# Routed attention and an ELU layer on one core: v asked for ahead of k, k kept in x's columns, weight conversion dealt out by spare time

## The chip, the cores and the metric

The kernel runs on one core of one Trainium2 chip. The metric is the time of one execution in device microseconds (us). Durations and waits below come from one profiled execution.

## The reference, cut to what matters

```python
# q, k, v: (4, 8, 768, 64) float32; centroids: (8, 16, 64) float32
q_assign = argmax(einsum('bhsd,hcd->bhsc', q_n, c_n)); k_assign = argmax(einsum(... k_n, c_n))
scores = where(q_assign == k_assign, q @ k.T / 8, -1e9)        # per batch and head
x = (softmax(scores) @ v)                                       # 4*768 = 3072 tokens x 512
h = x @ w_in                                                    # w_in: (512, 2048)
out = where(h > 0, h, exp(min(h, 0)) - 1) @ w_out               # w_out: (2048, 512)
```

The two weights arrive as float64, so the kernel itself has to turn them into float32.

## The kernel before, in words

**Attention.** The work is cut into 32 *slots*: for each of 4 batches, 2 halves of 384 queries, and 4 pairs of heads (`blocks`, line 153). `slot(n)` (line 555) records one slot on all engines in a fixed order; every engine runs its own instructions in the order recorded. In slot n TensorE does the row sums of slot n-2 (`row_sums`, L500, `d_bank`), the product with v of slot n-1 (`values`, L482, `o_bank`), in some slots the match of the next queries or keys with the centroids (`similar`, L373), and then for six blocks of keys the scores (`plain`, L444) and the cluster mask added to them (`masked`, L457), in a ring of three PSUM tiles. ScalarE takes the exponentials of the six score tiles (L466) into `p_out`, which has one buffer: the first exponential of slot n+1 overwrites what VectorE adds up in `sums_begin` (L469) of slot n. VectorE's queue in a slot holds `sums_end` of slot n-1 (L474, L475), `divide` of slot n-2 (L514, L515), `assign` where clusters are matched (L386 to L399), transposes of the next batch's k and q (L580, L587, L591), then `weigh(n)` (line 595), then `sums_begin` of slot n (L469). GpSimd multiplies x by the reciprocal sums (L518) and makes the query masks (L409).

**Loads.** SyncE's queue issues all loads. In each slot it holds the k loads (`load_k`, 4 transfers for each pair of heads) or the q loads (`load_q`, 16 transfers) of the next batch first, and behind them `load_v(n + 1)` (line 594). v has two buffers, so the v of slot n+1 may be written once `values(n - 1)` has read the buffer. At the start SyncE asks for the centroids, the first q, the first k (8 transfers), v of slot 0, the other half of q, and then four pieces of weights (L300).

**Weight conversion.** The weights are cut into 16 pieces of 1 MB (8 of w_in, then 8 of w_out). A piece is loaded as words into a *place*: `words_w` (to the end), two places in columns of `xT` and one in `spare` (the last three only up to some piece). `begin` is two VectorE instructions (L319, L327) and one for ScalarE behind the slot's exponentials (L329, through `later` and `flush`); `join` is three VectorE instructions (L338, L341, L344). After them the place is free, and `ask` (line 279) records the load of the next piece into it. A table `order` written by hand says which slot has a begin ("b") or a join ("j"). It runs on through four more steps, the four *units* of the first group of the second stage: pieces 13, 14 and 15 are begun and joined there.

**Second stage.** Tokens come in six groups of 512. Each group has four units (`unit`, L666: seven block products with w_in, summed in a way that saves the eighth) and a `second_product` with w_out (L758). Sums of blocks are needed as operands: of x (`x_sums`, L627 to L630, GpSimd), of w_in (`sum_low`, L639, and `w_step`, L646 to L650, GpSimd) and of w_out (`weight_sums`, L814 to L817, VectorE, once, in the first group after its four units). In a unit VectorE adds m5 to a bank (L713), which TensorE's sixth product then adds to, and u3 to another (L723); the rest of a unit's VectorE work (`rest_of`) stands at the start of the next.

## Time and profile before

| | us |
|---|---|
| median of three runs (987.08 to 990.1) | 989.21 |
| the profiled execution, its own time | 989.96 |
| its span | 988.2 |
| TensorE busy in the span | 933.7 |
| VectorE, ScalarE, GpSimd busy | 530.3, 371.1, 279.8 |

The span runs from 0 to 988.2. The slots end near 373.6, the first group of the second stage runs to 496.6, and the other groups take 96.7 each. In a timeline row the first number is the start, the second the duration in us; then come engine, line, operation, tiles, how many instructions the row merges, and in brackets how long the engine had been idle and what ended that. SPq is SyncE's queue, whose rows are the issuing of transfers and not their data. PEclk is the clock that TensorE was granted, in tenths.

### The profile page before, as it was taken

The numbers are of one execution on the slowest core, as the hardware profiler recorded it, in microseconds if no ns is written. First come the engines' busy times: TensorE is split into PE (matmuls) and PEld (weight loads), VectorE is DVE, ScalarE is ACT, GpSimd is POOL, SyncE is SP. The second block draws the span as 40 slices with busy tenths as digits, with TensorE's granted clock in tenths as the row PEclk, the third lists the DMA queues.
The fourth block names the chain that finished last, engine by engine and source line by source line (L and its number), as shares of the span: only waits on it lengthen the run. The fifth ranks groups of instructions, "written<-read, shape, count | busy, mean of one in ns | idle before, by whom it ended". The sixth has DMA issues, their size and how long they took to land.

```text
span 988.2 us, 12274 instructions
## 1 busy us (share of the span) xinstructions
PE 933.7 (94%) x4905; PEld 674.8 (68%) x4907; DVE 530.3 (54%) x638; ACT 371.1 (38%) x619; POOL 279.8 (28%) x251
## 2 busy tenths in 40 slices
PE   6699999999899979877999999999999999999996
PEld 3244444444344437766888888888888888888885
DVE  4768899889788986756134213422441244214321
ACT  3567877577577754320033103300330032003200
POOL 1102020221203174627034504440444043405200
PEclk9899999999999989987999999999999999999999
DMA  6853535434322211110000000000000100010001
GB/s 141 238 139 81 119 69 117 121 73 109 79 76 91 76 59 43 45 41 1 22 22 1 1 21 22 1 1 24 20 1 1 42 1 1 0 43 1 1 1 45
DMA packets 107983, 49.13 MB, mean 50 GB/s; under 512 B 93200, under 2 KB 101392, under 8 KB 107280
## 3 DMA queue, kind: packets, MB, share of 16 engines
q1 hardware_dynamic: 107920, 48.28, 18.5%
q8 instruction: 40, 0.66, 0.3%
q14 instruction: 23, 0.19, 0.1%
HBM read 41.98 MB, written 6.29 MB: 49 GB/s over the span
## 4 chain that ended last, share of the span: by engine, by line
PE 80%; DVE 9%; issue 3%; DMA 3%; SPq 3%; POOL 1%; ACT 1%; DVEq 0%; POOLq 0%
PE bank L758 29%; PE bank L666 21%; PE o_bank L482 10%; PE banks L444 9%; PE o_bank L666 4%; SPq L163 3%; PE banks L457 2%; PE d_bank L666 2%; PE d_bank L500 2%; DMA kq_g<-in_v_dram 2%; DVE sums_w L474 1%; PE d_bank L373 1%; DMA words_w<-in_moe_w_out_dram 1%; DVE sums_w L469 1%; POOL kq_g L677 1%
## 5 line engine op out<-in xcount | busy, mean ns | idle before, releaser
L758 PE MATMUL bank<-w_out,kq_g 128*128 128x256 f32 x768 | 172.0, 384 | 8.4 <-DVE w_out L815 8.4
L758 PEld LDWEIGHTS bank<-w_out,kq_g 128*128 128x128 f32 x768 | 148.0, 193 | 29.2 <-DVE w_out L815 8.5
L466 ACT ACTIVATE p_out<-banks 128x768 f32<-128x768 f32 x192 | 154.6, 812 | 27.8 <-PE banks L457 27.7
L482 PE MATMUL o_bank<-p_out,kq_g 128*64 128x384 f32 x768 | 135.3, 503 | 14.9 <-DMA kq_g<-in_v_dram 14.9
L482 PEld LDWEIGHTS o_bank<-p_out,kq_g 128*64 128x64 f32 x768 | 56.4, 142 | 89.2 <-issue 66.5
L677 POOL TENSOR_SCALAR kq_g<-kq_g 128x512 f32<-128x512 f32 x96 | 63.1, 667 | 170.0 <-ACT kq_g L676 169.8
L680 DVE SCALAR_TENSOR_TENSOR kq_g<-kq_g,bank 128x512 f32<-128x512 f32 x72 | 49.4, 686 | 115.3 <-POOL kq_g L677 115.3
L518 POOL TENSOR_TENSOR xT<-xT,sums_w 128x384 f32<-128x384 f32 x32 | 36.7, 1146 | 228.7 <-DVE sums_w L515 212.6
L666 PE MATMUL bank<-xT,w_in 128*128 128x256 f32 x384 | 90.7, 379 | 0.1
L646 POOL TENSOR_TENSOR spare<-w_in 128x512 f32<-128x512 f32 x24 | 33.5, 1395 | 179.9 <-PE bank L666 177.0
L666 PEld LDWEIGHTS bank<-xT,w_in 128*128 128x128 f32 x384 | 73.0, 190 | 10.1
L666 PE MATMUL bank<-xT,spare 128*128 128x256 f32 x288 | 69.7, 394 | 7.3 <-ACT bank L712 4.0
L469 DVE TENSOR_TENSOR sums_w<-p_out 128x1536 f32<-128x1536 f32 x32 | 57.1, 1786 | 21.0 <-ACT p_out L466 21.0
L666 PE MATMUL bank<-x_sum,w_in 128*128 128x256 f32 x288 | 68.0, 379 | 0.0
L666 PEld LDWEIGHTS bank<-xT,spare 128*128 128x128 f32 x288 | 56.8, 198 | 16.3 <-POOL kq_g L677 8.1
L474 DVE TENSOR_TENSOR sums_w<-sums_w,p_out 128x1536 f32<-128x1536 f32 x32 | 58.3, 1823 | 3.3
L666 PEld LDWEIGHTS bank<-x_sum,w_in 128*128 128x128 f32 x288 | 54.7, 190 | 7.4
L676 ACT ACTIVATE kq_g<-bank 128x512 f32<-128x512 f32 x72 | 42.0, 598 | 38.6 <-PE bank L666 36.9
L705 ACT COPY bank<-bank 128x512 f32<-128x512 f32 x12 | 6.8, 570 | 125.3 <-PE bank L666 125.3
L409 POOL TENSOR_SCALAR kq_g<-w_out,big,minus 128x768 bf16<-128x768 bf16 x16 | 28.6, 1793 | 72.3 <-ACT w_out L402 72.3
L444 PE MATMUL banks<-kq_g 64*128 64x384 f32 x192 | 41.8, 515 | 5.3 <-ACT p_out L466 5.3
L758 PE MATMUL bank<-sums_w,p_out 128*128 128x256 f32 x192 | 42.4, 379 | 0.0
(162 smaller groups left out, 1388.3 us busy)
## 6 DMA issues: line engine op xcount, KB each, us to landing
kq_g<-in_v_dram SPq DMA_DIRECT2D x32, 384.0 KB, 3.4
words_w<-in_moe_w_out_dram SPq DMA_DIRECT2D x6, 1024.0 KB, 5.1
out_dram<-p_out SPq DMA_DIRECT2D x24, 256.0 KB, 2.3
w_out<-in_q_dram SPq DMA_DIRECT2D x112, 48.0 KB, 2.4
w_out<-in_k_dram SPq DMA_DIRECT2D x48, 96.0 KB, 3.2
words_w<-in_moe_w_in_dram SPq DMA_DIRECT2D x3, 1024.0 KB, 5.6
xT<-in_moe_w_in_dram SPq DMA_DIRECT2D x3, 1024.0 KB, 8.5
spare<-in_moe_w_in_dram SPq DMA_DIRECT2D x2, 1024.0 KB, 10.2
```

The costliest lines, as they stand in the source:

```text
L444: nc.tensor.matmul(s[:, e, :HS], lhsT=kT[b % 2][pr][rows, ts(kt, P)], rhs=qT[half][pr][rows], start=True, stop=False,)
L466: nc.scalar.activation(probs[kt], s[:, :, :HS], Act.Exp, scale=SCALE)
L469: nc.vector.tensor_tensor(add_to, probs_all[:, : 4 * HS], probs_all[:, 4 * HS : 8 * HS], op=Alu.add)
L474: nc.vector.tensor_tensor(add_to, add_to, probs_all[:, 8 * HS :], op=Alu.add)
L482: nc.tensor.matmul(o_bank[64 * e : 64 * e + 64, :HS], lhsT=v_raw[n % 2][:, e, kt], rhs=probs[kt][:, e], start=(kt == 0), stop=(kt == NT - 1),)
L518: nc.gpsimd.tensor_tensor(x_of(n), x_of(n), r_of, op=Alu.mult)
L646: nc.gpsimd.tensor_tensor(s2, s1, a11, op=Alu.subtract)
L666: nc.tensor.matmul(bank[:, ts(f, QS)], lhsT=left[:, ch, ts(f, P)], rhs=right[:, ch], start=first and f == 0 and ch == 0, stop=ch == 1, ski ...
L676: nc.scalar.activation(to, bank.rearrange("p (f n) -> p f n", f=2), Act.Exp)
L677: nc.gpsimd.tensor_scalar(to, to, 1.0, 0.0, op0=Alu.min, op1=Alu.max)
L680: nc.vector.scalar_tensor_tensor(to, to, -1.0, bank.rearrange("p (f n) -> p f n", f=2), op0=Alu.add, op1=Alu.max)
L758: nc.tensor.matmul(bank[:, ts(i, QS)], lhsT=left[:, f, ts(i, P)], rhs=right[:, f], start=first and f == 0 and i == 0, stop=f == half - 1, ...
```

## The change

Six things are changed.

1. `load_v(n + 1)` stands ahead of a slot's k and q loads.
2. The first k is asked for by ScalarE: four transfers as its first instructions, four more after its second table load. Its copies out of PSUM are shared by ScalarE and VectorE, the centroids are transposed after q, and the mask columns of the second half of k are copied by ScalarE after the first three exponentials of slot 0.
3. k of batches 0 and 2 is kept in the last 768 columns of `xT` rather than in the first 3072 columns of `w_out`'s tile (`early`). The places for words are now `words_w`, the first 2048 columns of `early` (for pieces 0 to 7) and `spare` (to piece 9); for piece 13 alone there is one more, the last 2048 columns of `early`, from slot 25 on.
4. The table `order` is replaced by a rule: each slot brings an amount of spare time (`ROOM`), unused time is carried on up to 2.5, and begin, join and sum steps are taken in order as long as the credit pays their `COST`. A join is now three steps that may fall into different slots, and the place is given back after the second of them. By this rule all 16 pieces are begun by slot 30 and joined by slot 31 but for the last step of piece 15 (after unit 0).
5. The sums of w_out are four steps of the same list: three after unit 2, one after unit 3. Tiles `words_w` and `sums_w` change roles in them.
6. `sum_low` is gone: after slot 25 GpSimd issues two transfers from `w_in` into `w_in` that add as they write. The first group's x sums and w sums are dealt over slots 27 to 30, where they stood together after slot 30.

The core of the diff:

```diff
-        [early[:, ts(pr, S)] for pr in range(NPR)],
+        [xT[:, pr, N - S :] for pr in range(NPR)],
...
-    first_k = [
-        rows_of(t, k[0, 2 * pr : 2 * pr + 2])
-        for pr, t in enumerate(raw_k + kT[1][2:])
-    ]
+    def load_first_k(pr):
+        first_k[pr] = rows_of(nc.scalar, (raw_k + kT[1][2:])[pr], k[0, 2 * pr : 2 * pr + 2])
+
+    load_first_k(0)
+    load_first_k(1)
     load_v(0)
     load_q(0, 1)
...
     nc.scalar.preload_act_table_set("natural_log_exp_and_others")
+    load_first_k(2)
+    load_first_k(3)
...
-    places += [(xT[:, 2 * n : 2 * n + 2, N - WC :], 6) for n in range(KC // 2)]
-    places += [(spare.rearrange("p a n -> p (a n)")[:, : 2 * WC].unsqueeze(1), into + 4)]
+    places += [(early[:, : 2 * WC].unsqueeze(1), into)]
+    places += [(spare.rearrange("p a n -> p (a n)")[:, : 2 * WC].unsqueeze(1), into + 2)]
...
-        order[n] = ("", "j", "b", "j", "b", "", "j", "b")[n % NB]
...
+        [2.3, 2.6, 3.0, 3.0, 1.4, 1.7, 2.6, 2.6] * (B - 1)
...
+    COST = {"begin": 1.4, "join": 1.25, "sum": 2.2}
...
+        credit = min(credit, 2.5) + ROOM[n]
+        begun = False
+        while steps and credit >= COST[steps[0][0]]:
+            kind, m = steps[0]
+            if kind == "join" and begun or kind == "sum" and n < len(blocks) + 2:
+                return
...
-        nc.scalar.copy(kT[0][pr].rearrange("p (h s) -> p h s", h=2), ps[:, :, :HS])
+        copy = nc.vector.tensor_copy if pr % 2 else nc.scalar.copy
+        copy(kT[0][pr].rearrange("p (h s) -> p h s", h=2), ps[:, :, :HS])
...
-    for other in told:
-        other()
+    told[0]()
     flush()
+    told[1]()
...
+        if n + 1 < len(blocks):
+            load_v(n + 1)
         if at == 0:
             nc.vector.transpose(qT_all[1], raw_q_all)
...
-        if n + 1 < len(blocks):
-            load_v(n + 1)
         weigh(n)
...
-            if k_ == 0:
-                sum_low(u + 1)
             w_step(u + 1, 0)
...
-        if n == last_n - 1:
-            x_sums(0, nc.gpsimd)
-            sum_low(0)
-            for m in range(3):
-                w_step(0, m)
+        if n == 3 * NB + 1:
+            places.append((early[:, 6144:].unsqueeze(1), into + 6))
+            ask()
+            for ch in range(2):
+                nc.gpsimd.dma_start(
+                    w_in[:, ch, DF // 2 :], w_in[:, 2 + ch, DF // 2 :], accum_op=Alu.add
+                )
+        elif last_n - 4 <= n < last_n:
+            x_sum_step(0, n - last_n + 4)
+            if n > last_n - 4:
+                w_step(0, n - last_n + 3)
```

Three places show how the instructions move. The first is SyncE's queue from the first q to slot 1. `in_q`, `in_k`, `in_v` and `in_moe_w_in` are the inputs in memory, `kq_g` holds v's two buffers, and `words_w`, `xT`, `w_out` and `spare` hold places for words. Before:

```order
L189 DMA p_out<-in_q_dram 128x3x64 x8
L189 DMA w_out<-in_k_dram 128x6x64 x4
L189 DMA kq_g<-in_k_dram 128x6x64 x4
L179 DMA kq_g<-in_v_dram 128x2x384
L163 DMA w_out<-in_q_dram 32x12x32 x16
L300 DMA words_w<-in_moe_w_in_dram 128x2048
L300 DMA xT<-in_moe_w_in_dram 128x2x1024 x2
L300 DMA spare<-in_moe_w_in_dram 128x2048
L163 DMA w_out<-in_k_dram 32x24x32 x8
L179 DMA kq_g<-in_v_dram 128x2x384
L163 DMA w_out<-in_q_dram 32x12x32 x16
```

And after, the same stretch of SyncE's queue:

```order
L189 DMA p_out<-in_q_dram 128x3x64 x8
L179 DMA kq_g<-in_v_dram 128x2x384
L163 DMA w_out<-in_q_dram 32x12x32 x16
L303 DMA words_w<-in_moe_w_in_dram 128x2048
L303 DMA w_out<-in_moe_w_in_dram 128x2048
L303 DMA spare<-in_moe_w_in_dram 128x2048
L179 DMA kq_g<-in_v_dram 128x2x384
L163 DMA w_out<-in_k_dram 32x24x32 x8
L179 DMA kq_g<-in_v_dram 128x2x384
L163 DMA w_out<-in_q_dram 32x12x32 x16
```

The first k has left the queue, three pieces of weights are asked for where there were four, and the v of slot 1 stands ahead of the next batch's k.

The second place is VectorE in slot 30, with slot 29's `sums_begin` ahead of it. Before:

```order
L469 TENSOR_TENSOR sums_w<-p_out 128x1536
L474 TENSOR_TENSOR sums_w<-sums_w,p_out 128x1536
L475 TENSOR_TENSOR sums_w<-sums_w 128x768
L514 TENSOR_TENSOR sums_w<-sums_w 128x384
L515 SCALAR_TENSOR_TENSOR sums_w,r_sum<-sums_w 128x384
L338 SCALAR_TENSOR_TENSOR sums_w<-words_w,sums_w 128x1024
L341 SCALAR_TENSOR_TENSOR w_out<-words_w,w_out 128x1024
L344 SCALAR_TENSOR_TENSOR w_out<-w_out,sums_w 128x1024
L319 TENSOR_SCALAR w_out<-words_w 128x1024
L327 TENSOR_SCALAR sums_w<-words_w 128x1024
L469 TENSOR_TENSOR sums_w<-p_out 128x1536
```

And after, where the join is of piece 14 and the begin of piece 15:

```order
L510 TENSOR_TENSOR sums_w<-p_out 128x1536
L515 TENSOR_TENSOR sums_w<-sums_w,p_out 128x1536
L516 TENSOR_TENSOR sums_w<-sums_w 128x768
L555 TENSOR_TENSOR sums_w<-sums_w 128x384
L556 SCALAR_TENSOR_TENSOR sums_w,r_sum<-sums_w 128x384
L342 SCALAR_TENSOR_TENSOR sums_w<-words_w,sums_w 128x1024
L346 SCALAR_TENSOR_TENSOR w_out<-words_w,w_out 128x1024
L352 SCALAR_TENSOR_TENSOR w_out<-w_out,sums_w 128x1024
L322 TENSOR_SCALAR w_out<-words_w 128x1024
L330 TENSOR_SCALAR sums_w<-words_w 128x1024
L510 TENSOR_TENSOR sums_w<-p_out 128x1536
```

The rows are the same: both times a join out of `words_w` is followed at once by a begin out of `words_w`, with the load of the next piece between them.

The third place is VectorE at the border of units 2 and 3 of the first group. Before, with the join of piece 14 and the begin that waits for the words of piece 15:

```order
L713 TENSOR_TENSOR bank_2403<-bank_2403,spare 128x512
L680 SCALAR_TENSOR_TENSOR kq_g<-kq_g,bank_2402 128x2x256
L723 TENSOR_TENSOR bank_2405<-bank_2405,spare 128x512
L338 SCALAR_TENSOR_TENSOR sums_w<-words_w,sums_w 128x1024
L341 SCALAR_TENSOR_TENSOR w_out<-words_w,w_out 128x1024
L344 SCALAR_TENSOR_TENSOR w_out<-w_out,sums_w 128x1024
L319 TENSOR_SCALAR w_out<-words_w 128x1024
L327 TENSOR_SCALAR sums_w<-words_w 128x1024
L680 SCALAR_TENSOR_TENSOR kq_g<-kq_g,bank_2403 128x2x256
```

And after:

```order
L757 TENSOR_TENSOR bank_2423<-bank_2423,spare 128x512
L724 SCALAR_TENSOR_TENSOR kq_g<-kq_g,bank_2422 128x2x256
L765 TENSOR_TENSOR bank_2425<-bank_2425,spare 128x512
L362 TENSOR_TENSOR sums_w<-w_out 128x2048
L364 TENSOR_TENSOR w_out<-w_out 128x8x256
L366 TENSOR_TENSOR sums_w<-w_out,sums_w 128x2048
L724 SCALAR_TENSOR_TENSOR kq_g<-kq_g,bank_2423 128x2x256
```

Join and begin have given way to three sums of w_out, which wait for no load; the four sums that stood after unit 3 are no longer there.

More of the change, by code (lines that the diff above doesn't have):

```diff
@@ L532, in main_path @@
                 nc.vector.tensor_copy(qT[0][pr], ps[:, e, :HS])
-    told = clusters_q(0, 0, d_bank)
-    told()
+    nc.tensor.transpose(o_bank[:, :P], work[:, : 2 * D], ident)
+    nc.vector.tensor_copy(cT, o_bank[:, :P])
+    clusters_q(0, 0, d_bank)()
     flush()
```

121 lines of the change are left out of this document (73 added, 48 removed).

## The prediction

> **What bounds the kernel now.** I read the page's slices first, then the busy time by stage, then who waited for whom, then the timeline of the engine that waits.
>
> ```profile
> PE   6699999999899979877999999999999999999996
> ```
>
> TensorE is busy nearly throughout; the slices that fall short lie in the first 20, that is, before about 494. The busy times of three stretches (TensorE's comes first, VectorE's third; then the granted clock) say how much is there.
>
> ```profile
> 53.20:373.60 320.40, 307.51 (x2018) 141.77 (x2016) 284.07 (x315) 226.17 (x367) 72.00 (x49) 0.98 0.37 93
> 373.60:496.60 123.00, 107.18 (x459) 91.15 (x460) 66.31 (x74) 24.41 (x43) 51.62 (x37) 0.92 0.08 30
> 496.60:593.30 96.70, 96.70 (x449) 85.13 (x449) 30.19 (x39) 19.79 (x35) 31.85 (x32) 1.00 0.03 12
> ```
>
> The second group of the second stage (third row) has no wait at all: 96.70 busy of 96.70, at full clock. The first group does the same products in 123.00, so 26.3 us of it are waits and slow clock. From the second group on nothing can be gained by this change, which leaves that work alone. The rest of the loss lies in the slots, and the waits name it.
>
> ```profile
> PE o_bank L482 <- DMA kq_g<-in_v_dram: 14.9, 4, 7.3
> PE bank L758 <- DVE w_out L815: 8.4, 1, 8.4
> PE banks L444 <- ACT p_out L466: 8.1, 2, 5.3
> PE bank L666 <- POOL kq_g L677: 3.3, 1, 3.3
> ```
>
> So TensorE waits four times for v, twice for exponentials, and in the first group for the sums of w_out and once for GpSimd.
>
> **v ahead of k (a gain).** TensorE's timeline around those four waits, with an undisturbed slot between them:
>
> ```profile
> 46.60 6.65 PE L482 MATMUL o_bank<-p_out,kq_g 128*64 128x384 f32 x24 [7.35 <-DMA kq_g<-in_v_dram]
> 67.94 0.87 PE L500 MATMUL d_bank<-sums_w,ones 128*64 128x384 f32 x4
> 68.64 4.04 PE L482 MATMUL o_bank<-p_out,kq_g 128*64 128x384 f32 x24
> 77.65 0.87 PE L500 MATMUL d_bank<-sums_w,ones 128*64 128x384 f32 x4
> 90.58 4.09 PE L482 MATMUL o_bank<-p_out,kq_g 128*64 128x384 f32 x24 [1.57 <-DMA kq_g<-in_v_dram]
> 174.16 5.79 PE L482 MATMUL o_bank<-p_out,kq_g 128*64 128x384 f32 x24 [2.54 <-DMA kq_g<-in_v_dram]
> 260.40 2.19 PE L482 MATMUL o_bank<-p_out,kq_g 128*64 128x384 f32 x6 [3.50 <-DMA kq_g<-in_v_dram]
> ```
>
> An undisturbed slot lasts 77.65 - 67.94 = 9.71, and its product with v 4.04. After the waits of 7.35 and 2.54 that product takes 6.65 and 5.79, at a slower clock: 2.6 and 1.75 more; after 1.57 it does not (4.09). For the fourth wait, longer than the third, I take the third's 1.75. The four cost 14.9 + 2.6 + 1.75 + 1.75 = 21.0.
>
> Why v is late stands in SyncE's queue:
>
> ```profile
> 27.25 14.82 SPq L163 DMA_DIRECT2D w_out<-in_k_dram  x8
> 42.11 0.65 SPq L179 DMA_DIRECT2D kq_g<-in_v_dram  x1
> 76.18 10.60 SPq L163 DMA_DIRECT2D w_out<-in_q_dram  x16
> 86.88 8.21 SPq L179 DMA_DIRECT2D kq_g<-in_v_dram  x3
> ```
>
> Eight k transfers take 14.82 to be asked for, and v only then, at 42.11; it is wanted near 39 and its product starts at 46.60. Later, v stands behind sixteen q transfers (10.60). With v first, each is asked for some 10 us earlier, and the largest wait was 7.35, so all four go: -21.0. What v is moved past comes later instead: v's request waits until the product of the slot before last has read the buffer, some 5 us into the slot (0.7 + 4.04), and k or q behind it by as much. They are turned two or three slots later, 19 us or more, so this costs nothing; if that cover were gone it would be up to 5 us in a slot.
>
> **Conversion dealt out: the slots.** Pieces 13 to 15 move into the slots. Their prices, from VectorE's timeline:
>
> ```profile
> 97.86 1.18 DVE L338 SCALAR_TENSOR_TENSOR sums_w<-xT,sums_w 128x1024 uint32<-128x1024 uint32 x1
> 101.35 1.75 DVE L469 TENSOR_TENSOR sums_w<-p_out 128x1536 f32<-128x1536 f32 x1
> 107.02 0.58 DVE L386 STREAM_TRANSPOSE w_out<-d_bank 128x384 f32<-128x384 f32 x1
> 109.32 0.65 DVE L319 TENSOR_SCALAR w_in<-xT 128x1024 uint32<-128x1024 uint32 x1
> 110.49 1.75 DVE L469 TENSOR_TENSOR sums_w<-p_out 128x1536 f32<-128x1536 f32 x1
> ```
>
> A join runs from 97.86 to 101.35, 3.49; the fixed sums of a slot from there to 107.02, 5.67; matching clusters to 109.32, 2.30; a begin to 110.49, 1.17. Joins that meet GpSimd's multiplication, which the divide ahead of them sets off, are dearer (the second step 2.02 below, where a third of 3.49 is 1.2), about 4.3. Three more pieces are 3 x 5.5 = 16.5, so VectorE goes from 284.07 to about 300 in a stretch that without v's waits lasts some 309. It fits on the whole, by 8 us, and the rule keeps each slot near its spare 9.71 - 5.67 = 4.0. I put the moved joins at nothing, with the cover of 8 us named; without it see the second rival.
>
> One wait stays. In slot 30 the rows before and after are the same: a join frees `words_w`, the next piece is loaded into it, and the begin stands right behind.
>
> ```profile
> 348.73 1.22 DVE L338 SCALAR_TENSOR_TENSOR sums_w<-words_w,sums_w 128x1024 uint32<-128x1024 uint32 x1
> 349.87 2.02 DVE L341 SCALAR_TENSOR_TENSOR w_out<-words_w,w_out 128x1024 f32<-128x1024 uint32 x1
> 356.94 1.29 DVE L319 TENSOR_SCALAR w_out<-words_w 128x1024 uint32<-128x1024 uint32 x1 [2.84 <-DMA words_w<-in_moe_w_out_dram]
> 359.82 2.85 DVE L469 TENSOR_TENSOR sums_w<-p_out 128x1536 f32<-128x1536 f32 x1
> 359.94 1.15 ACT L329 ACTIVATE sums_w<-sums_w,off 128x1024 uint32<-128x1024 uint32 x1 [8.02 <-DVE sums_w L327]
> 363.63 1.65 PE L444 MATMUL banks<-kq_g 64*128 64x384 f32 x4 [5.28 <-ACT p_out L466]
> ```
>
> The load takes 356.94 - 351.89 = 5.05. Join and begin last 359.82 - 348.73 = 11.1; queued behind them are VectorE's sum and ScalarE's L329 with all its exponentials, and TensorE waits 5.28, then loses about 2.6 to the clock as after the 7.35: 7.9. After the change GpSimd's eight sums no longer fall into the begin (359.82 - 356.94 = 2.88 there, 1.17 alone): 1.7 less. Slots 27 to 29 bring the steps of before in another order (5.5, 4.3 and 1.2 where 4.3, 1.2 and 5.5 stood), which would bring VectorE to slot 30 earlier, and two of GpSimd's sums each, which slow it; I take the two as cancelling. The wait is then 5.28 - 1.7 = 3.6, and its clock loss, between the 1.75 after 2.54 and the 2.6 after 7.35, about 2.2: 5.8, a gain of 2.1 (bounds: all 7.9 gained, or 3 lost).
>
> The Trainium skill ("TensorE: Matmul & The Clock Gate", "Part 1: The HAM clock gate") says that the clock falls to half after an idle window of about 3.4 us. This trace slows after 2.54 already, so a wait between 2.5 and 3.4 would cost 1.75 by the trace and nothing by the page.
>
> **Conversion and sums: the first group (a gain).** Two of the places where the 26.3 us go, and what the sums of w_out cost:
>
> ```profile
> 424.00 0.69 DVE L319 TENSOR_SCALAR w_out<-words_w 128x1024 uint32<-128x1024 uint32 x1 [3.66 <-DMA words_w<-in_moe_w_out_dram]
> 428.07 3.75 PE L666 MATMUL bank<-xT,spare 128*128 128x256 f32 x8 [4.00 <-ACT bank L712]
> 451.88 4.63 PE L758 MATMUL bank<-w_out,kq_g 128*128 128x256 f32 x10 [8.40 <-DVE w_out L815]
> ```
>
> VectorE waits for words at 424.00; behind it stand its additions to the banks, and TensorE waits 4.00 at 428.07 (and 3.3 in the unit before, with GpSimd between). The four sums then hold it for 8.40: 15.7 together. The remaining 10.5 are 107.18 busy against 96.70: slow clock after these waits and 0.9 of row sums. After the change no load and no begin is left here. What stays: the row sums, 0.9, about as much again for the first unit's start (an estimate), and a new, smaller wait, for three sums now stand between L723 of unit 2 and the L713 of unit 3. The same two units of the second group, undisturbed:
>
> ```profile
> 530.11 0.70 DVE L723 TENSOR_TENSOR bank<-bank,spare 128x512 f32<-128x512 f32 x1 [0.38 <-ACT spare L721]
> 538.73 0.70 DVE L713 TENSOR_TENSOR o_bank<-o_bank,spare 128x512 f32<-128x512 f32 x1 [1.61 <-ACT bank L712]
> 541.32 1.89 PE L666 MATMUL o_bank<-xT,spare 128*128 128x256 f32 x8
> ```
>
> VectorE is free at 530.8. A sum of 2048 columns is 1.75 x 2048/1536 = 2.33, three are 7.0, and 1.6 more if two of GpSimd's operations meet them at the 0.8 of above; the rest of the unit behind them is five operations of 0.7, and L713 another 0.7: done at 543.6. TensorE wants it at 541.32: it waits 2.3 (0 to 3.5), and I add half of 1.75 for the clock. The first group lasts 96.7 + 1.8 + 2.3 + 0.9 = 101.7: -21.3 (bounds -18 to -24.5).
>
> **The block added by a transfer.** No row shows such a transfer; the nearest are 1 MB loads. It is issued after slot 25 and first needed by the w sums after slot 28, about 29 us later, on GpSimd, behind which x's multiplications are queued. At nothing it is hidden by those 29 us; GpSimd is rid of four sums of blocks, for which TensorE never waited longer than the 3.3 above.
>
> **First k by ScalarE (a loss).**
>
> ```profile
> 6.44 0.48 ACT L530 COPY x_sum<-banks 128x384 f32<-128x384 f32 x1 [1.68 <-PE banks L526]
> 6.56 2.69 SPq L189 DMA_DIRECT2D w_out<-in_k_dram  x4
> 25.07 4.40 ACT L466 ACTIVATE p_out<-banks 128x768 f32<-128x768 f32 x6
> ```
>
> No row shows ScalarE asking. By SyncE's row four requests take 2.69, and two such groups, 5.4, now stand in ScalarE's queue ahead of its copy of q at 6.44. ScalarE has some of that time free (1.68 just ahead of the copy), so I let the copy move by 2.4 (bounds 0 and 5.4), and all that follows with it. Sharing the k copies, and putting half of the mask copies behind three exponentials, gives most of it back by the first exponential (25.07), but that half, about 1.0, then stands among the six. Net +1.5 (-1.5 if requests cost ScalarE nothing, +3.4 if nothing is given back). SyncE's later loads are asked for that much sooner, which only v needs.
>
> The Trainium skill ("DMA: Bandwidth & Descriptors", "Issuing engines are not separate DMA queues") says that asking from several engines saves only the time to ask. By the page this part could gain no more than that time; the row gives it as 2.69 for four, and it is not saved but moved to ScalarE.
>
> **Sum.** -21.0 - 2.1 - 21.3 + 1.5 = -42.9. The profiled execution took 989.96, its span 988.2 and 1.8 around it; it would come to 947.1. It lies 0.75 above the median, 989.21, and against that I forecast 946.
>
> **Rivals.**
> 1. *The left waits go too* (0.12): slot 30's load lands in time and the sums hide behind the unit. For it: an exponential of the next slot needs VectorE's sum only some 5 us into that slot. Against: the same rows in slot 30. 5.8 + 3.2 less: 937.
> 2. *VectorE becomes the bound of the slots* (0.18): if GpSimd's work meets each step, as it did at 349.87, eight joins of w_in and sixteen begins cost 0.8 more each: 19, of which 8 is covered: 11 more, 957. For it: 300 of 309. Against: the join quoted above cost 3.49.
> 3. *v does not come sooner at the start* (0.10), so the change does less than it says: three pieces of weights are still ahead of the first v. The queue stood 14.82 over eight k requests with four pieces ahead; if the data and not the asking was the limit, and is still, the 10 us of the first wait stay: 956. Against: one piece and all of k have gone from ahead of v.
> 4. *The adding transfer is late* (0.03), slower than before: GpSimd stops at the first w sum, and x's multiplications behind it, ScalarE and TensorE follow within a slot. It decides from 29 + 43 = 72 us after its issue; at 100 us the kernel takes 946 + 71 = 1017. Against: the slowest group of loads of 1 MB lands 10.2 after its issue in the median:
>
> ```profile
> spare<-in_moe_w_in_dram SPq DMA_DIRECT2D x2, 1024.0 KB, 10.2
> ```
>
> The Trainium skill ("SBUF — State Buffer", "SBUF: two separate sides") says that a transfer issued from GpSimd can stand while VectorE holds the port through which GpSimd writes its descriptors. No run here shows one.
>
> **How the numbers follow.** My forecast has 0.57, the rivals 0.12, 0.18, 0.10 and 0.03. The range 936 to 961 holds the first three rivals and the bounds of slot 30, of the start and of the first group, each by itself; outside lie the fourth rival and several bad bounds at once. A difference under 0.3% (3 us) can't be told from none. Faster 0.96, same 0.01, slower 0.03.
>
> **What would show it.** In the new profile: no wait of the product with v, and slots of 9.71 (more where clusters are matched) from slot 1 to 29; one wait of TensorE for an exponential near slot 31, of 2 to 6; a first group of 100 to 104 with a wait in unit 3; the first exponentials at 25 to 27. It is wrong if the slots grow beyond 9.71 with VectorE busy throughout, if v's wait is back in slot 2, or if GpSimd waits for its transfer.

## The result and the profile after

The kernel after takes **956.02 us** (median of 4 runs, 955.51 to 957.19), the kernel before 988.14 in the runs beside it (986.79 to 990.1): a ratio of 0.9675, with a 95% interval of 0.9653 to 0.9697. That is 32 less where the forecast was 43 less. It lies inside the range given, but in the sum behind it one term has the wrong sign and one is far too small, while two hold. The profiled execution took 955.51, of which the span is 953.7.

TensorE's row of the slices is the first thing to set beside the one of before: the short slices of the slots have gone, but for the very first and one 7, from 334 to 358, where slot 30 lies.

```profile
PE   3999999999999979999999999999999999999996
```

The first digit was 6 and is 3, and that is about the start. The loads and waits of five stretches say the rest (TensorE's busy time first, VectorE's third, then the granted clock): the start up to the first product with v, the slots, the last slots, the first group of the second stage, and the second group.

```profile
0.00:35.40 35.40, 18.09 (x97) 10.31 (x97) 16.00 (x41) 10.71 (x17) 2.70 (x9) 1.00 0.96 223
35.40:307.00 271.60, 271.60 (x1830) 126.16 (x1828) 261.26 (x304) 207.08 (x334) 61.53 (x42) 1.00 0.48 117
307.00:361.00 54.00, 45.65 (x288) 20.79 (x284) 50.00 (x42) 30.79 (x53) 23.10 (x12) 0.94 0.21 70
...
361.32:462.10 100.78, 99.08 (x460) 85.63 (x459) 44.41 (x58) 21.64 (x40) 39.28 (x34) 1.00 0.02 6
462.10:558.80 96.70, 96.70 (x449) 85.13 (x449) 30.20 (x39) 19.78 (x35) 31.78 (x32) 1.00 0.03 12
```

From 35.4 to 307 TensorE has no idle time at all and VectorE is busy 261 of 272. In the last slots TensorE lacks 8.35 and some clock; in the first group 1.7.

**The start.** Before, TensorE reached the first product with v at 28.54:

```profile
28.54 4.09 PE L482 MATMUL o_bank<-p_out,kq_g 128*64 128x384 f32 x24
```

ScalarE's queue after, from the first instruction, and that product on TensorE:

```profile
0.76 4.51 ACTq L189 DMA_DIRECT2D w_out<-in_k_dram  x4
...
6.81 1.28 ACT L242 ACT_TABLE_LOAD   x1
10.12 4.12 ACTq L189 DMA_DIRECT2D kq_g<-in_k_dram  x4
14.29 0.48 ACT L571 COPY x_sum<-banks 128x384 f32<-128x384 f32 x1 [6.19 <-DMA w_out<-in_q_dram]
35.41 4.09 PE L523 MATMUL o_bank<-p_out,kq_g 128*64 128x384 f32 x24
```

Four requests take ScalarE 4.51 and 4.12, and between the table load, done at 8.09, and the second four stands a gap of 2.03, for which the rows name no reason. The first copy of q (L571; it was L530) starts at 14.29 instead of 6.44, and the product with v at 35.41: **6.9 later**, where 1.5 was forecast.

**The slots.** Three lines of TensorE's waits after; none of its waits names v any more. (`L485` is the old `L444`, `L507` the exponentials, `L757` the additions to the banks.)

```profile
PE banks L485 <- ACT p_out L507: 8.9, 4, 6.0
PE banks L567 <- ACT x_sum L571: 8.4, 2, 7.8
PE o_bank L710 <- DVE o_bank L757: 1.7, 1, 1.7
```

The first blank matmul behind attention starts at 361.32 instead of 373.63, 12.3 sooner. The slots can be read from the starts of TensorE's row sums, one in each slot. Before, those of slots 27, 30 and 31; after, those of slots 27 to 31:

```profile
321.85 0.87 PE L500 MATMUL d_bank<-sums_w,ones 128*64 128x384 f32 x4
...
350.99 0.87 PE L500 MATMUL d_bank<-sums_w,ones 128*64 128x384 f32 x4
368.73 1.10 PE L500 MATMUL d_bank<-sums_w,ones 128*64 128x384 f32 x4
```

```profile
307.16 0.87 PE L541 MATMUL d_bank<-sums_w,ones 128*64 128x384 f32 x4
318.40 0.87 PE L541 MATMUL d_bank<-sums_w,ones 128*64 128x384 f32 x4
329.48 0.87 PE L541 MATMUL d_bank<-sums_w,ones 128*64 128x384 f32 x4
339.19 0.87 PE L541 MATMUL d_bank<-sums_w,ones 128*64 128x384 f32 x4
356.65 0.87 PE L541 MATMUL d_bank<-sums_w,ones 128*64 128x384 f32 x4
```

From the first product with v to the row sums of slot 27 it is 293.3 before (28.54 to 321.85) and 271.75 after (35.41 to 307.16): **21.6 gained** for v, against 21.0. A slot is 9.71. Before, slot 30 was too long by 8.0 (17.74), and slot 31 took 0.2 more to the blank matmul (4.90, where after has 4.67); after, slots 27, 28 and 30 are too long, by 1.53, 1.37 and 7.75, together 10.65: **2.4 more**, where 2.1 less was forecast. With the 6.9 of the start, 21.6 - 2.4 - 6.9 makes up the 12.3.

VectorE, ScalarE and TensorE around the long slot:

```profile
339.48 1.22 DVE L342 SCALAR_TENSOR_TENSOR sums_w<-words_w,sums_w 128x1024 uint32<-128x1024 uint32 x1
340.62 2.02 DVE L346 SCALAR_TENSOR_TENSOR w_out<-words_w,w_out 128x1024 f32<-128x1024 uint32 x1
342.67 2.18 DVE L352 SCALAR_TENSOR_TENSOR w_out<-w_out,sums_w 128x1024 f32<-128x1024 f32 x1
347.67 0.70 DVE L322 TENSOR_SCALAR w_out<-words_w 128x1024 uint32<-128x1024 uint32 x1 [2.82 <-DMA words_w<-in_moe_w_out_dram]
349.00 1.15 ACT L332 ACTIVATE sums_w<-sums_w,off 128x1024 uint32<-128x1024 uint32 x1 [8.89 <-DVE sums_w L330]
352.54 1.65 PE L485 MATMUL banks<-kq_g 64*128 64x384 f32 x4 [5.99 <-ACT p_out L507]
```

From the join's start to the end of the begin, at 348.9, it is now 9.4 instead of 11.1, as forecast. But the join starts 0.3 behind the slot's row sums (339.19), where before it started 2.3 ahead of them (348.73 and 350.99): VectorE comes to it 2.5 later, not sooner.

**The first group** lasts 100.78 instead of 122.97: **22.2 gained**, against 21.3. VectorE's sums of w_out, the next addition to a bank, and TensorE behind it, in units 2 and 3:

```profile
397.48 2.28 DVE L362 TENSOR_TENSOR sums_w<-w_out 128x2048 f32<-128x2048 f32 x1
399.79 2.58 DVE L364 TENSOR_TENSOR w_out<-w_out 128x2048 f32<-128x2048 f32 x1
402.29 2.69 DVE L366 TENSOR_TENSOR sums_w<-w_out,sums_w 128x2048 f32<-128x2048 f32 x1
409.11 0.69 DVE L757 TENSOR_TENSOR o_bank<-o_bank,spare 128x512 f32<-128x512 f32 x1
409.94 1.97 PE L710 MATMUL o_bank<-xT,spare 128*128 128x256 f32 x8 [1.70 <-DVE o_bank L757]
```

The three sums end at 404.98, 7.5 behind their start, and the one wait that is left is 1.70, in unit 3, where 2.3 was forecast; its clock loss is small (1.97 for a product of 1.89).

The four parts, -21.6, +2.4, -22.2 and +6.9, add up to -34.5, the difference of the two spans (988.2 and 953.7). It is more than the 32 of the medians because the profiled execution of before, 989.96, was one of its longer ones, and that of after its shortest.

### The profile page after: what moved, and what is told of

It is laid out like the page before. It is cut to its first block, busy times and chain, and to the rows that moved or that the text cites. A ratio compares the mean times of both kernels' runs of the same rounds, so it can differ in the third digit from the quotient of the medians.

```text
span 953.7 us, 12273 instructions
## 1 busy us (share of the span) xinstructions
PE 918.4 (96%) x4907; PEld 668.3 (70%) x4907; DVE 523.1 (55%) x640; ACT 369.1 (39%) x617; POOL 274.9 (29%) x249
## 3 DMA queue, kind: packets, MB, share of 16 engines
q1 hardware_dynamic: 101264, 46.71, 18.5%
## 4 chain that ended last, share of the span: by engine, by line
PE 81%; DVE 13%; DMA 2%; ACT 1%; SPq 1%; issue 1%; DVEq 0%; ACTq 0%
PE bank L796 30%; PE bank L710 23%; PE banks L485 8%; PE o_bank L523 8%; PE o_bank L710 4%; DVE sums_w L515 2%; PE banks L498 2%; PE d_bank L710 2%; PE d_bank L541 2%; DVE sums_w L510 2%; DVE sums_w L516 1%; SPq L163 1%; DVE w_out L352 1%; PE d_bank L414 1%; DVE w_out L346 1%
## 5 line engine op out<-in xcount | busy, mean ns | idle before, releaser
L796 PE MATMUL bank<-w_out,kq_g 128*128 128x256 f32 x768 | 169.0, 379 | 0.0
L507 ACT ACTIVATE p_out<-banks 128x768 f32<-128x768 f32 x192 | 153.7, 813 | 27.6 <-PE banks L498 22.5
L796 PEld LDWEIGHTS bank<-w_out,kq_g 128*128 128x128 f32 x768 | 145.8, 190 | 19.8
L523 PE MATMUL o_bank<-p_out,kq_g 128*64 128x384 f32 x768 | 129.3, 486 | 0.0
L710 PE MATMUL bank<-xT,spare 128*128 128x256 f32 x288 | 66.1, 379 | 0.0
L515 DVE TENSOR_TENSOR sums_w<-sums_w,p_out 128x1536 f32<-128x1536 f32 x32 | 61.0, 1907 | 3.7 <-ACT sums_w L551 0.5
L710 PEld LDWEIGHTS bank<-xT,spare 128*128 128x128 f32 x288 | 54.7, 190 | 7.4
L450 POOL TENSOR_SCALAR kq_g<-w_out,big,minus 128x768 bf16<-128x768 bf16 x16 | 35.0, 2193 | 64.6 <-ACT w_out L443 64.6
L485 PE MATMUL banks<-kq_g 64*128 64x384 f32 x192 | 41.3, 510 | 8.3 <-ACT p_out L507 8.3
L796 PE MATMUL bank<-sums_w,kq_g 128*128 128x256 f32 x192 | 42.4, 379 | 0.0
```

Of the source, the lines that this page charges most:

```text
L450: nc.gpsimd.tensor_scalar(q_mask[half][:, :, x], hot_q, big[:, x : x + 1], minus[:, x : x + 1], op0=Alu.mult, op1=Alu.add,)
L485: nc.tensor.matmul(s[:, e, :HS], lhsT=kT[b % 2][pr][rows, ts(kt, P)], rhs=qT[half][pr][rows], start=True, stop=False,)
L507: nc.scalar.activation(probs[kt], s[:, :, :HS], Act.Exp, scale=SCALE)
L515: nc.vector.tensor_tensor(add_to, add_to, probs_all[:, 8 * HS :], op=Alu.add)
L523: nc.tensor.matmul(o_bank[64 * e : 64 * e + 64, :HS], lhsT=v_raw[n % 2][:, e, kt], rhs=probs[kt][:, e], start=(kt == 0), stop=(kt == NT - 1),)
L710: nc.tensor.matmul(bank[:, ts(f, QS)], lhsT=left[:, ch, ts(f, P)], rhs=right[:, ch], start=first and f == 0 and ch == 0, stop=ch == 1, ski ...
```

## The experiments

The kernels ran in five sets, each on one chip with runs of the kernel before in between; these had medians of 986.45 to 989.05, so a difference of 1 to 2 between kernels of two sets tells nothing. The medians, and the ratios to the kernel before in the same set (the sets are parted by the empty rows):

| kernel | median us | ratio (95%) |
|---|---|---|
| the change | 956.02 | 0.9675 (0.9653 to 0.9697) |
| | | |
| first k by SyncE | 953.33 | 0.9669 (0.9639 to 0.9700) |
| second k group behind the copies | 949.81 | 0.9623 (0.9602 to 0.9643) |
| begin not in the slot of its load | 951.11 | 0.9629 (0.9604 to 0.9653) |
| before, with v ahead alone | 968.54 | 0.9803 (0.9770 to 0.9835) |
| | | |
| first k by GpSimd | 953.91 | 0.9658 (0.9636 to 0.9680) |
| k by SyncE, first begin in slot 1 | 946.81 | 0.9581 (0.9560 to 0.9603) |
| sums of w_out at the end | 964.15 | 0.9756 (0.9734 to 0.9778) |
| lower block added by GpSimd | 957.13 | 0.9686 (0.9664 to 0.9708) |
| | | |
| first begin in slot 1 alone | 954.81 | 0.9676 (0.9651 to 0.9701) |
| three edits together | 940.75 | 0.9535 (0.9510 to 0.9560) |
| the three, joins spread | 940.18 | 0.9527 (0.9502 to 0.9552) |
| | | |
| as the last, k by GpSimd | 944.28 | 0.9561 (0.9541 to 0.9581) |

The theory to be tested: the sum fell short by the start (ScalarE's queue) and by the last slots (a begin behind its own load); its rivals are that transfers, whoever asks for them, set the start, and that VectorE as a whole sets the last slots.

### First k by SyncE again

```diff
-    load_first_k(0)
-    load_first_k(1)
+    for pr in range(NPR):
+        load_first_k(pr)
     load_v(0)
...
-        first_k[pr] = rows_of(nc.scalar, (raw_k + kT[1][2:])[pr], k[0, 2 * pr : 2 * pr + 2])
+        first_k[pr] = rows_of(nc.sync, (raw_k + kT[1][2:])[pr], k[0, 2 * pr : 2 * pr + 2])
```

> The changed kernel with one part undone: SyncE asks for all eight transfers of the first k again, behind the first q and ahead of v. Theory A (asking holds ScalarE: its two groups of requests, 4.51 and 4.12 with a gap of 2.03 ahead of the second, stand ahead of its first copy of q, which starts at 14.29 instead of 6.44): the copy is back between 6.4 and 7.5, the first product with v starts at 29 to 30 instead of 35.41, and the kernel takes 950 (949 to 951.5) instead of 956. Theory B (the transfers themselves fill the DMA engines from 4 us on, whoever asks): the first product with v stays near 35, and the kernel takes 955 to 958.

Measured: 953.33, between the two (its runs spread from 951.53 to 956.95). ScalarE's first copy, the first product with v, and what came behind:

```profile
5.56 0.48 ACT L569 COPY x_sum<-banks 128x384 f32<-128x384 f32 x1 [0.86 <-PE banks L565]
29.12 2.16 PE L521 MATMUL o_bank<-p_out,kq_g 128*64 128x384 f32 x12
31.44 1.15 ACT L330 ACTIVATE sums_w<-sums_w,off 128x1024 uint32<-128x1024 uint32 x1 [5.41 <-DVE sums_w L328]
33.34 2.27 PE L521 MATMUL o_bank<-p_out,kq_g 128*64 128x384 f32 x12 [2.06 <-ACT p_out L505]
```

The copy and the product are back where theory A wants them, 6.3 sooner. But SyncE now gets to the words at 24.55 instead of 19.23, the first begin waits for them in slot 0, and its step on ScalarE (L330) stands ahead of exponentials that the product needs: TensorE waits 2.06 in the middle of it. From 25.5 to 29.1 the granted clock was 0.53 as well. So asking from ScalarE did buy something, 5.3 of SyncE's time, which the forecast had put at nothing.

### The second k group behind the copies of q

```diff
     nc.scalar.preload_act_table_set("natural_log_exp_and_others")
-    load_first_k(2)
-    load_first_k(3)
...
+    load_first_k(2)
+    load_first_k(3)
     nc.tensor.transpose(o_bank[:, :P], work[:, : 2 * D], ident)
```

> The changed kernel with ScalarE's second group of four k requests behind its two copies of the first q instead of ahead of them. Theory A: the first copy starts at about 8.2, when the table load ends; the second group is then asked for from about 10.8 to 15 and lands near 19, where its transposes would want it near 17, so the first product with v starts at 31 to 32.5 and the kernel takes 952.5 (951.5 to 954). Theory B (the transfers fill the DMA engines): 955 to 958.

Measured: 949.81, more than theory A hoped for, because the second group landed all but in time (its transposes wait 0.4).

```profile
8.01 0.48 ACT L569 COPY x_sum<-banks 128x384 f32<-128x384 f32 x1
11.61 2.81 ACTq L189 DMA_DIRECT2D kq_g<-in_k_dram  x4
29.80 4.09 PE L521 MATMUL o_bank<-p_out,kq_g 128*64 128x384 f32 x24
```

The copy starts as the table load ends, and the product at 29.80, 5.6 sooner than in the change. The place of four requests ahead of two copies, with the gap ahead of them, thus cost 5.6. Behind the copies the same four requests took 2.81, not 4.12.

### No begin in the slot of its load

```diff
+        first_unasked = asked
+        fresh = range(first_unasked, len(pieces))
         while steps and credit >= COST[steps[0][0]]:
             kind, m = steps[0]
+            if kind == "begin" and m in fresh:
+                return
```

> The changed kernel with one rule more in the dealing out: a block of words isn't begun in the slot in which it was asked for, so that the begin of block 15 moves from slot 30 to slot 31 and its three joins behind the first unit of the first group. Theory A (TensorE's wait of 5.99 in slot 30 is the begin's wait for words, with the exponentials queued behind it): the wait goes, slot 30 lasts 9.7 to 10.5 instead of 17.46, up to 2 comes back in the first group, and the kernel takes 949.5 (948 to 951). Theory B (VectorE is late by the three joins of each of the slots 27, 28 and 30 anyway, and the 2.82 that it waits for words is all there is to gain): 953 (952.5 to 954).

Measured: 951.11, between the two. The wait of 5.99 is gone, and in the same slot this one stands:

```profile
348.54 1.09 PE L489 MATMUL banks<-kq_g 64*128 64x384 f32 x4 [2.02 <-ACT p_out L511]
```

This slot lasts 13.7 instead of 17.46 and not 9.7 to 10.5: 3.8 of its 7.75 go with the begin that waits for its load. Of the 4.0 that are left, 2.02 are this wait: the exponentials stand behind VectorE's fixed sum, which comes late by the joins, as theory B has it, and takes 2.83. The other 2 are slow clock (0.62 granted from 348.5 to 353; the next products take 1.50 for 0.81). The first group still has only its wait of 1.7, so the joins of block 15 that moved there cost nothing.

### The kernel before with v ahead, alone

```diff
+        if n + 1 < len(blocks):
+            load_v(n + 1)
         if at == 0:
...
-        if n + 1 < len(blocks):
-            load_v(n + 1)
         weigh(n)
```

> The kernel before with one part of the change alone: in each slot v is asked for ahead of k and q. Theory A (v is late because it is asked for late): its four waits go with the slow clock behind them, 21 in all, and the kernel takes 967 (965 to 969) instead of 988. Theory B (three pieces of weights still stand ahead of the first v, and their data fill the DMA engines): the first wait of 7.35 and its 2.6 stay, 977.

Measured: 968.54 against 987.0, 18.5 less (16.3 to 22.7 by the interval), and 21.9 less by the profiled spans (988.2 and 966.3). From the first product with v (29.94) to the row sums of slot 27 (301.91) it is 272.0, 21.3 less than before. No product waits for v any more. Theory A.

### First k by GpSimd

```diff
-        first_k[pr] = rows_of(nc.scalar, (raw_k + kT[1][2:])[pr], k[0, 2 * pr : 2 * pr + 2])
+        first_k[pr] = rows_of(nc.gpsimd, (raw_k + kT[1][2:])[pr], k[0, 2 * pr : 2 * pr + 2])
```

with all four pairs asked for at the place of the first two.

> The changed kernel with all eight transfers of the first k asked for by GpSimd, which has no work until 15 or later, instead of ScalarE. Theory A (what ScalarE loses is only the place of its requests ahead of its copies): the first copy of q comes at 5.6 to 6.5, SyncE still gets to its words 5.3 sooner than when it asks for k itself, the first product with v starts at 29 to 30, and the kernel takes 949.5 (948.5 to 950.5). Theory B (k beside q on the DMA engines delays q: the first transposes began at 6.16 and 6.24 in the two kernels in which ScalarE asked, at 4.65 when SyncE asked for everything): the first copy comes near 7 and the product with v at 30 to 31, 950.5 to 952. If GpSimd asks much more slowly than 1.1 for each, k is late for its transposes near 13, and it is 953 or more.

Measured: 953.91, none of the three reasons given. GpSimd also makes the identity matrix, and its requests now stood ahead of that:

```profile
8.09 0.22 POOL masks.py:197 MEMSET ident<- 128x128 f32 x1
8.74 0.90 PE L565 MATMUL banks<-ident,p_out 128*128 128x128 f32 x3 [8.74 <-POOL off L258]
```

The same mistake as the change's, on another engine: the requests were priced, not what was queued behind them. It leaves the question of the transfers open; the last experiment puts it again.

### Where the start's loss lies: the first begin

The first begin moves to slot 1, with k by SyncE in one kernel and as in the change in the other.

```diff
+    ROOM[0] = 0.0
     credit, later = 0.0, []
```

> The kernel in which SyncE asks for the first k, with the first block of words begun in slot 1 and not in slot 0. Theory A (there the first words, asked for at 24.55 instead of 19.23, were late for the begin of slot 0, and ScalarE's exponentials stood behind it: 2.06 of waiting and a slow clock): the wait goes, slot 2 starts at 38.9 to 39.8 instead of 41.37, and the kernel takes 950 (949 to 951) instead of 953.3. Theory B (the slow clock of the first slot and the late rest come from transfers that fill the DMA engines): no change, 953.

> The changed kernel with the first begin in slot 1 instead of slot 0 and nothing else; ScalarE still asks for the first k. Theory A (ScalarE's asking is the late start; its words land in time for slot 0, so that begin costs only what ScalarE's L332 of 1.15 takes ahead of the exponentials): the product with v still starts at 35 and the kernel takes 955 (954 to 956). Theory B (most of the 9.2 between the changed kernel and the one with SyncE asking and the begin in slot 1 is the begin's): 948 to 951.

Measured: 946.81 and 954.81. Without k by SyncE the edit brings 1.2 against the change, which can't be told from nothing across two sets; with it 6.5. The first product with v in the two kernels, SyncE's first:

```profile
27.32 4.09 PE L522 MATMUL o_bank<-p_out,kq_g 128*64 128x384 f32 x24
```

```profile
35.09 4.09 PE L524 MATMUL o_bank<-p_out,kq_g 128*64 128x384 f32 x24
```

So 7.8 of the start are ScalarE's asking, the place of its requests and k's travelling beside q together. The rest of the change's edits there, above all the copies of k shared with VectorE and half of the mask copies behind three exponentials, brought 28.54 to 27.32, 1.2; no run takes these edits alone. That the kernel with k by SyncE gained 3.2 more than expected is for 1.8 the clock ahead of that product (27.32 and 29.12): 1.00 from 25.5 to 29.1, where it had been 0.53. TensorE's wait ahead of that stretch, 0.86 and 0.87, was the same in both; the rows don't tell why the clock fell in one, nor is the rest of the 3.2 traced (the runs of the first SyncE kernel spread over 5.4).

### The sums of w_out at the end

```diff
-            if kind == "join" and begun or kind == "sum" and n < len(blocks) + 2:
+            if kind == "join" and begun or kind == "sum" and n < len(blocks) + 4:
```

> The changed kernel with the four sums of w_out at the end of the first group, where the kernel before had them, the conversion still in the slots. Theory A (dealing them into units 2 and 3 trades a wait of 8.4 for one of 1.70): TensorE waits 8 to 9 at the second product's first matmul that needs them and loses 0.7 to 1.8 to the clock, the 1.70 in unit 3 goes, and the kernel takes 963.5 (962 to 965.5). Theory B (the conversion in the first group was what delayed the sums, and VectorE now comes to them early enough): the wait is under 5 and the kernel takes 957 to 960.

Measured: 964.15, theory A: the wait in unit 3 is gone and the old one is back to the tenth.

```profile
PE bank L796 <- DVE w_out L364: 8.4, 1, 8.4
```

### The lower block added by GpSimd

```diff
+            if k_ == 0:
+                sum_low(u + 1)
             w_step(u + 1, 0)
...
-            for ch in range(2):
-                nc.gpsimd.dma_start(
-                    w_in[:, ch, DF // 2 :], w_in[:, 2 + ch, DF // 2 :], accum_op=Alu.add
-                )
...
+            if n == last_n - 4:
+                sum_low(0)
```

> The changed kernel with the lower block of w_in added by GpSimd in four sums, as in the kernel before, instead of by the transfer. Theory A (the transfer landed 13 after its issue and nobody waited for it; four sums of about 1.3 are spare time of GpSimd): 956 to 957. Theory B (GpSimd's chain in the first group was what made TensorE wait 3.3 in the kernel before, and the transfer is what took that wait away): a wait of 2 to 4 for GpSimd or what stands behind it comes back in a unit, 959 to 961.

Measured: 957.13, 0.13 above theory A's range, and theory A by its trace: no wait for GpSimd came back, and the first group's only wait is the 1.7 in unit 3. In the change's own trace the transfer lands 10.7 to 12.8 after its issue.

```profile
L877 POOL DMA_DIRECT2D w_in<-w_in x2: 1001/1072/1144, 295.7 to 296.5; - x2
...
DMA to landing us min/median/max: 10.7/11.7/12.8
```

It was allowed 29. The part is worth nothing that can be measured, either way.

### The edits together

Three edits: k by SyncE, the first begin in slot 1, no begin in the slot of its load.

> SyncE asks for the first k, the first begin stands in slot 1, and no block is begun in the slot in which it was asked for. Theory A (the start and the slot with the late words are two separate losses): the gains of 9.2 and 4.9 add up, no wait of TensorE over 2.5 is left from slot 1 on, and the kernel takes 942 (941 to 943.5). Theory B (VectorE's work in the last slots is the common limit and takes back what comes sooner): 944 to 946.5.

Measured: 940.75, just under theory A's range: the gains add up, and TensorE's longest wait in the slots is 1.8. Then fewer steps of joins in each of the last slots:

```diff
-        + [2.3, 2.6, 4.0, 4.0, 3.0, 3.0, 3.0, 3.0]
+        + [2.3, 2.6, 4.0, 2.5, 2.5, 2.5, 2.5, 2.5]
```

> As the kernel with all three edits, with less room given to the slots from 27 on (2.5 each instead of 4.0 and four of 3.0), so that at most two joins stand in one of these slots and the rest moves into the first group. Theory A (three joins in a slot, 5.3 beside GpSimd's sums, are what leaves waits of 0.6 to 2 there): the waits go, VectorE's few joins more in the first group are hidden, and the kernel takes 939.5 (938.5 to 941). Theory B (GpSimd's sums slow VectorE's fixed sums too, 2.82 where 1.75 is usual, and the waits come from these): within 1 of the kernel without this edit. Theory C (the joins moved hold up an addition to a bank in the first group): slower than it by 1 to 3.

Measured: 940.18, 0.6 less. The time alone fits theory A too (938.5 to 941); the waits decide for theory B. TensorE's waits for exponentials, without and with the last edit:

```profile
PE banks L488 <- ACT p_out L510: 3.0, 3, 1.8
```

```profile
PE banks L488 <- ACT p_out L510: 3.4, 4, 1.6
```

They are not fewer. With at most two steps of joins in a slot VectorE's fixed sums beside GpSimd still take 2.8, and a begin there 3.1 instead of 1.2:

```profile
310.84 1.49 DVE L320 TENSOR_SCALAR w_out<-words_w 128x1024 uint32<-128x1024 uint32 x1
312.25 1.76 DVE L328 TENSOR_SCALAR sums_w<-words_w 128x1024 uint32<-128x1024 uint32 x1
313.94 2.85 DVE L513 TENSOR_TENSOR sums_w<-p_out 128x1536 f32<-128x1536 f32 x1
```

This is the fastest version here by its median, 4.7% less than the kernel before, though the 0.6 can't be told from nothing. That what waits it has left in the last slots come from GpSimd's x and w sums is what these rows suggest; moving those was not tried.

### k beside q, with nothing behind the requests

In this fastest version GpSimd asks for the first k, behind the identity matrix and its other memsets.

```diff
     nc.gpsimd.memset(off, -896.0 * 2**23)
+    for pr in range(NPR):
+        load_first_k(pr)
```

> The fastest kernel so far (940.2) with the first k asked for by GpSimd, this time behind the identity matrix and its other memsets, so that nothing waits behind the requests. Theory A (who asks matters only through what stands behind the requests): the first transposes begin at 4.7 to 5, the first product with v at 27.2 to 28, and the kernel takes 940 to 941. Theory B (k travelling beside q delays q, as when ScalarE asked: first transposes at 6.2): the first product with v is at 28.5 to 30.5 and the kernel takes 941.5 to 943.5.

Measured: 944.28, beyond theory B. No engine's queue is held up, and yet TensorE waits four times for the first q, and the first product with v starts at 31.83 instead of 27.44:

```profile
PE banks L570 <- DMA p_out<-in_q_dram: 10.6, 4, 6.1
```

The time from issue to landing of the eight transfers of the first q: in the kernel with k by SyncE, in the change, and here.

```profile
p_out<-in_q_dram SPq DMA_DIRECT2D x8, 96.0 KB, 2.6
```

```profile
p_out<-in_q_dram SPq DMA_DIRECT2D x8, 96.0 KB, 4.1
```

```profile
p_out<-in_q_dram SPq DMA_DIRECT2D x8, 96.0 KB, 5.7
```

With k behind it in one queue q lands in 2.6; with k asked for on a second queue in the same microseconds it lands later. The Trainium skill ("DMA: Bandwidth & Descriptors", "Issuing engines are not separate DMA queues") says that transfers of all issuing engines run on the same sixteen engines and interleave; the trace agrees, as far as landing times can show it, with 2.6, 4.1 and 5.7. Why it is more from GpSimd stays open: there all eight transfers of k are asked for beside q (1.53 to 8.3), in the change only the first four (0.76 to 5.27), and the traces count GpSimd's eight as 512 packets, ScalarE's as 6272.

## Why the prediction was right or wrong

**What bounds the kernel, and v ahead of k: right.** The forecast was -21.0. The waits are gone, with 21.6 in the change's trace and 21.3 as the only edit. The third rival (data, not asking, makes the first v late) is refuted by that kernel: there all four pieces of weights were still ahead.

**The first group: right.** -22.2 against -21.3, with the wait in the unit that was named, 1.70 against 2.3. Putting the sums back at the end costs 8.1, and the wait is 8.4 again.

**The block added by a transfer: right**, at nothing. The fourth rival needed 72 to the landing; it took 13.

**First k by ScalarE: the step that failed most.** The prediction took SyncE's 2.69 as ScalarE's price for four requests, let the copy move by 2.4, and set the net at +1.5 with a bound of +3.4; it was +6.9. Three things were wrong. Four requests took 4.51 and 4.12, and the second four began 2.0 behind the end of the table load. The second four stood right ahead of the copies: that alone is 5.6. The first four held the table loads, which end at 8.09 and, with k by SyncE, at 4.69. And the transfers were not looked at: k beside q made q's landing 4.1 instead of 2.7 and the first transposes start at 6.16 instead of 5.55. The rows don't part what the first four cost from what q's landing did; together it is about 2. What was right is the size of the give-back, 1.2 for all other edits of the start (the sum had 0.9 for it). The sentence that SyncE's earlier loads help v alone was wrong as well: the first begin needs its words from there, and without them waits.

**The last slots: the sign was wrong, by 4.5.** The wait in slot 30 was named, its place too, and its shorter join and begin (9.4 against 11.1). Two steps failed. The first is "I put the moved joins at nothing": slots 27 and 28, 9.71 before, became 1.53 and 1.37 too long, 2.9 together, because TensorE waited 1.26 and 1.09 there for exponentials. The second is "I take the two as cancelling": VectorE came to slot 30 2.5 later, and that slot stayed 7.75 too long where the sum had 5.8. Slots 27 and 28 hold a whole join each, that is three steps. Beside GpSimd's x and w sums it took 5.3, where it took 4.3 beside GpSimd's multiplication alone and 3.5 with neither, and a fixed sum took 2.8 instead of 1.75. This is the second rival (VectorE as the bound of the slots), at about the price per step that it gave, but only in slots 27, 28 and 30, three of the four in which GpSimd has sums, not over all; from 35 to 307 the cover held. With the begin taken out of its load's slot 3.8 of the 7.75 go; the other half is VectorE's lateness and the slow clock behind the wait.

**The rule on the clock: a wait's length does not decide.** The prediction priced slow stretches by the length of the wait ahead of them, and did not look at one wait of its own trace: 2.83 for an exponential in slot 0, with the granted clock at 1.00 behind it. In the kernel before with v ahead alone the same wait of 2.83 stands at the same place, and behind it the clock was 0.53 from 26.8 to 30.0. A matmul row right behind the wait in the first trace, and one from the slow stretch of the second:

```profile
25.92 0.92 PE L444 MATMUL banks<-x_sum,w_out 64*128 64x384 f32 x4 [2.83 <-ACT p_out L466]
```

```profile
28.20 1.50 PE L444 MATMUL banks<-x_sum,w_out 64*128 64x384 f32 x4
```

A wait of 2.02 was followed by a slow stretch (no begin in the slot of its load), one of 2.06 was not (first k by SyncE), and at the change's start the clock stayed at 1.00 behind a wait of 7.78. So the 2.54 of the prediction is no threshold. The Trainium skill ("TensorE: Matmul & The Clock Gate", "Part 1: The HAM clock gate") gives an idle window of about 3.4. The traces do not bear it out as a threshold either, with slow stretches behind 2.02 and 2.54. What decides, these runs don't show. The 6.1 of slow clock that the sum counted behind the four waits for v came back with them.

The errors of the start (+5.4) and of the last slots (+4.5) make 9.9; the gains of v and of the first group were 0.6 and 0.9 larger than said. Together they are the 8.4 between -42.9 and -34.5. The total lies inside its range although the start lies outside its own bounds, and that it meets the 956 and 957 of the third and second rivals is chance: v does come sooner, and VectorE bounds three slots only. Two of the signs that the prediction named spoke against it, the slots 27 and 28 of 11.2 and 11.1 with VectorE busy throughout and the first exponentials at 30.75 instead of 25 to 27. The change as a whole is faster for the reasons given, and gives part of it back: with the asking undone and the two begins moved the kernel takes 940.75, 15 less.

## What to carry to other kernels

A request for a transfer is an instruction: before moving it to another engine, list what stands behind it in that queue, and ask what the transfer will travel beside. An engine with idle time at that place can still be the wrong one, if the idle time lies behind the request. When a planner gives out steps by their cost, take the cost from the stretch in which they will run, with the neighbours that run there, and keep a step that waits for a load out of the slot that starts the load.

## What the runs showed of the hardware

- Four requests of 192 KB, in rows of 256 bytes, kept ScalarE for 4.51 and 4.12 in the change and for 2.81 behind the copies, with SyncE asking beside it each time (3.76 to 4.42 in the other traces with ScalarE asking); SyncE took 2.69 to 3.63 for four, GpSimd 3.3 to 3.5. What sets ScalarE's price wasn't tried.
- A transfer asked for on a second queue took landing time from those asked for on the first in the same microseconds: the eight of q landed in 4.1 with four of k beside them from ScalarE and in 5.7 with eight from GpSimd, against 2.6 with k behind them.
- VectorE's instructions took 0.8 to 1.1 more each beside GpSimd's multiplications and sums: those of two inputs 2.02 and 2.18 for about 1.22, and 2.83 for 1.75, and one of the begin, of one input, 1.50 for 0.69. GpSimd's own sums took 2.25 for 1.26.
- The granted clock fell to 0.53 behind a wait of 0.87 in one profiled start and not in another with the same wait, and to 0.53 behind a wait of 2.83 in one trace and not in another.
